# Three moves in an attention and gated-feed-forward kernel: a Silu table load behind two copies, a value cast ahead of a key scaling, and store waits in the order of issue

## The chip, the cores and the metric

The kernel runs on one core of a Trainium2 chip. The metric is the device time of one execution in microseconds. The profile covers the span from the first to the last instruction of one execution; that span is a little shorter than the device time of the same run (271.1 us of 272.93).

## The reference

A linear attention over 8 batches and 8 heads of 576 positions with 64 elements each is followed by a feed-forward layer on the 4608 tokens:

```python
q_s = softmax(q, over the 64 elements)
k_s = softmax(k, over the 576 positions)
kv  = einsum('bhsd,bhse->bhde', k_s, v)
x   = einsum('bhsd,bhde->bhse', q_s, kv), as 4608 tokens x 512
h   = x @ w_in                                # 512 x 2048
g   = h / (1 + exp(-beta * h))                # beta: one per column of h
out = g @ w_out                               # 2048 x 512
```

Each softmax is an exponential divided by its sum (less the maximum, which the kernel does not need).

## The kernel before, in words

**Slabs and passes.** The tokens are worked in nine slabs. Slab t, for t from 0 to 7, holds the first 512 positions of batch t; slab 8 holds the 64 positions left over in each of the eight batches. Each slab has a first pass (x times w_in, 16 tiles of 128 columns, each of four matmuls into one PSUM bank, then a Silu on ScalarE at L746 that writes the bf16 tile GT and a scaling by 1/beta on VectorE at L769) and a second pass (GT times w_out). Slab 0 has a plain second pass (`pass2_group`). The others have `pass2_fast`, which splits the product into two by two blocks and forms them with seven block products in place of eight. These need sums and differences of blocks, made on VectorE (GS1, GS2, WSUM, and at L812 `g_diff`, which overwrites blocks of GT).

**The seven products and their banks.** In `pass2_fast` the products run at L846 in a fixed order on three PSUM banks, s, z5 and z2. After the fourth product z5 holds a finished output quarter, and after the fifth z2 does. ScalarE copies each to O2S (L882, `copy`). Then the sixth product adds to z5 and the seventh to z2, and VectorE adds each of these to TS and writes the last two quarters (L894, `last`). So the sixth and seventh product can't begin to accumulate before the copy of their bank is done. The seventh also reads a block that the second `g_diff` has overwritten.

**Attention.** It is worked one to two slabs ahead and placed between the matmuls of the slab in hand. For a batch: exponentials of q and k on ScalarE (L319), sums and reciprocals for q on VectorE (L357, L359), the product with the reciprocal (L361), a transposition of q, the cast of v to bf16 (`cast_v`, L377, tile VB), the product of keys and values (`kv_steps`), the reciprocal of the key sums (L490) and the scaling of kv with it into KVD (L449 or L459, the "key scaling"), and last the product of KVD and the transposed q, which is copied or cast to XT, the input of the next slab (L511 or L596). Batches 0 and 1 do this with a pair of heads (hp 0 to 3) at a time, from batch 2 on q is transposed by DMA (L606) and four output tiles come from `quad`, in two halves of two tiles (L554).

**What sets the order.** Each engine works its own instructions in the order in which the program adds them; waits between engines are put in by `Program` from what each operation reads and writes. The order is written by hand in two ways. In the first, a list `todo` holds pairs of a due time and a function; `tick` counts matmuls (a pass of a slab is 64 ticks for the first and 64 for the second), and a function is added to the program when its due time is reached. In the second, `pass2_fast` calls hooks: `at(n)` adds what was hung on point n with `on(n, ...)`. Point 4 comes after the copy of z5, point 5 after the copy of z2, point 6 after the addition of z5 and before the seventh product, point 7 at the end.

**ScalarE's table.** The exponential and Silu are in different table sets, and a switch is a table load. `silu_table` runs Silu on one element of a constant tile (DUMMY), so that the load (L1054) is made at that place of the queue and not ahead of the next slab's first real Silu. Slabs 1 and 2 use it in their second pass.

**The end.** The last slab's output goes out as ten stores (`store8`, L790), half issued by SyncE and half by ScalarE. After its last issue SyncE waits for every store's semaphore (L151), so that the program does not end before the data are out. There are twelve such semaphores: `out0` and `out1` for slabs 0 to 7, and ten whose names are built from the output quarter, the half and the tile, for instance `outr0011`.

The hooks of slab 2 and the due times of batch 1 in slab 0 are these lines:

```python
                todo += [(x, one(cast_v, 1, hp, DVE))
                         for hp, x in ((1, 118.5), (2, 123), (3, 127))]
                todo += [(x, steps(kv_steps, 1, (hp,), NOW))
                         for hp, x in enumerate((118, 122, 126))]
...
                on(4, exp_q, 4)
                on(4, silu_table)
                on(4, casts, 4)
                on(6, norm_turn, 4, 0)
```

Of the kernel before, what the change touches and what calls it, by code (L numbers as in the profile page):

```python
# [44 lines left out]
class Program:  # L45
# [83 lines left out]
    def emit(self, nc, es):  # L129
        counts, waits = self.plan()  # L130
        sems = {}
        for key in counts:
            sems[key] = es.enter_context(nc.semaphore("s_" + "_".join(str(x) for x in key)))
        by = {e: [] for e in (PE, ACTE, DVE, POOL, SP)}
        for op, w in zip(self.ops, waits):
            by[op.eng].append((op, w))

        def run(eng):
            def body(h):
                for op, w in by[eng]:  # L140
                    for key, n in w:
                        h.wait_ge(sems[key], n)
                    ins = op.fn(h)
                    if op.slot is not None:
                        ins.then_inc(sems[op.count[0]], 16)
                    elif op.inc:
                        ins.then_inc(sems[op.count[0]], 1)
                if eng == SP:
                    for key, n in sorted(counts.items(), key=str):
                        if key[0] == "dma" and str(key[1]).startswith("out"):  # L150
                            h.wait_ge(sems[key], n)  # L151
            return body

        with nc.Block() as blk:
            for e in (PE, ACTE, DVE, POOL, SP):
                getattr(blk, e)(run(e))


def bass_efficient_attn_shen__then__act_swish_beta_kernel(
# [12 lines left out]
    with ExitStack() as es:  # L172
# [343 lines left out]
        def outr_steps(b):  # L516
            pi = b // 2
            st = {}

            def one(hp, e_):  # L520
                if hp == 0 and e_ == 0:
                    st["b"] = bank()
                bk = st["b"]
                c = hp * 128 + e_ * 64
                d = kd(2 * pi + e_)
                mm(PS[bk][:, c:c + 64], KVD[d][:, hp, :], QTR[:, hp, 64 * e_:64 * e_ + 64],
                   True, True, r=[("kvd", d, hp), "qtr"], w=[("ps", bk)], bk=bk)
                if hp == 3 and e_ == 1:
                    o = bass.AP(XT8, pi * 128, [[NM * SM, 128], [SM, NM], [1, 128]])
                    add(DVE, lambda e: e.tensor_copy(o, PS[bk][:, :]), r=[("ps", bk)],  # L530
                        w=[("xt8", pi, 0), ("xt8", pi, 1)], bank=[bk])
            return [lambda hp=hp, e_=e_: one(hp, e_) for hp in range(NHP) for e_ in range(2)]
# [90 lines left out]
        def one(fn, *a):  # L623
            return lambda: fn(*a)

        def steps(fn, *a):
            return lambda: go(fn(*a))
# [4 lines left out]
        def attn(b):  # L632
            return [(24 if b == 5 else 16, steps(kv_all, b)),
                    (72, one(quad, b, (0, 1), b - 4))]

        def attn_late(b):
            if b < 4:
                x = 100 if b == 2 else 97
                return [(x, steps(kv_all, b)), (x + .1, lambda: g_diff(1)),
                        (118, one(quad, b, (0,)))]  # L640
            return [(96, steps(kv_all, b)), (99, lambda: g_diff(1)), (112, one(quad, b))]

        def spread(steps, lo, hi):
            return [(lo + (hi - lo) * k / len(steps), s) for k, s in enumerate(steps)]
# [310 lines left out]
        for t in range(NSLAB):  # L955
            todo = []
            if t == 0:
                todo = [(x, steps(t_steps, 1, (hp,), NOW, ACTE))
                        for hp, x in enumerate((97, 106, 114, 119))]
                todo += [(107, one(exp_kr_s, 1))]  # L960
                todo += [(x, one(exp_k, 1, hp, 1)) for hp, x in enumerate((108, 115, 120, 125.5))]
                todo += [(x, one(cast_v, 1, hp, DVE))
                         for hp, x in ((1, 118.5), (2, 123), (3, 127))]
                todo += [(x, steps(kv_steps, 1, (hp,), NOW))
                         for hp, x in enumerate((118, 122, 126))]
                todo += [(x, steps(out_step, 1, hp, NOW, ACTE)) for hp, x in enumerate((122.5, 125))]
                todo += [(117, one(o2_evac, 0, 0, 3, ACTE))]
                todo += [(2, steps(out_step, 0, 3, HEAD, DVE))]
            elif t < 4:
                todo = attn_late(t + 1)  # L970
                if t > 1:
                    todo += [(1.5, one(quad, t, (1,)))]
                if t == 3:
                    todo += [(4, one(norm_turn, 4, 2))]
                if t == 1:
                    todo += [(1, steps(out_step, 1, 2, (3,), ACTE)),
                             (3, steps(kv_steps, 1, (3,), (7,))),
                             (6, steps(out_step, 1, 3, (7,), DVE)),
                             (6.1, one(w_sum, 2, 4, 4)), (6.2, one(w_diff, 0)),
                             (6.3, one(w_diff, 1))]  # L980
            elif t < 7:
                todo = attn(t + 1)
            elif t == 7:
                todo = spread(outr_steps(1), 32, 48)
# [59 lines left out]
            def on(n, fn, *a):  # L1044
                hooks.setdefault(n, []).append(lambda: fn(*a))
# [18 lines left out]
            if t == 1:  # L1064
                on(0, exps, 2)
                on(0, casts, 2)
                on(2, norm_turn, 2, 0)
                on(3, norm_turn, 2, 2)
                on(3, g_diff, 0)
                on(4, silu_table)  # L1070
                on(3, load, 4)
            elif t == 2:
                on(0, exps, 3)
                on(2, norm_turn, 3, 0)
                on(3, norm_turn, 3, 2)
                on(3, g_diff, 0)
                on(3, load, 5)
                on(4, exp_q, 4)
                on(4, silu_table)
                on(4, casts, 4)  # L1080
                on(6, norm_turn, 4, 0)
            elif t == 3:
                on(0, exp_k, 4)
                on(0, exp_kr, 4)
                on(0, exp_q, 5)
                on(3, g_diff, 0)
                on(4, norm_turn, 5, 0)
                on(5, norm_turn, 5, 2)
                on(4, exp_qr, 1)
                on(5, exp_k, 5)  # L1090
                on(5, norm_turn_rem)
                on(5, casts, 5)
                on(5, load, 6)
                on(7, load_rem, "qrf", qt_h, QRF, 4)
            elif t + 2 < B:
                b = t + 2
                on(0, exps, b)
                on(0, casts, b)
                if t == 4:
                    on(0, load, 7)  # L1100
                on(3, norm_turn, b, 0)
                on(4, norm_turn, b, 2)
# [40 lines left out]
```

The softmax here doesn't subtract the row's maximum and nothing guards it: scores larger than these inputs give would overflow.

## Time and profile before

| | before |
|---|---|
| time, median of 3 runs | 272.82 us (272.47 to 272.95) |
| span of the profiled run | 271.1 us, 4991 instructions |
| TensorE busy | 262.9 us, 97% |
| VectorE busy | 192.1 us, 71% |
| ScalarE busy | 181.5 us, 67% |
| GpSimd busy | 64.0 us, 24% |
| mean granted TensorE clock | 0.998 |

Busy time is the sum over an engine's instructions; it says how full an engine is, not whether the end waited for it. The chain is the work that ended last, followed back from the last instruction to what released each step. The list of waits says which engine stood still, on which line, and which instruction of which engine it was waiting for. A wait of the busiest engine is a candidate for lost time; one of another engine usually is not. In the timeline each row has the start and the length in us, the engine, the line, the operation, and the tiles written and read; in brackets at the end is the idle time before it with what ended it. PE is TensorE, PEld its weight loads, DVE VectorE, ACT ScalarE, POOL GpSimd, SP SyncE; a q after the name is that engine's queue of instructions that are not compute.

### The profile page before, as it was taken

To read this page: it belongs to the slowest core of one execution; us is meant where nothing else is said; L and a number is where in the kernel's file an instruction comes from. 1 tells how busy PE (TensorE), PEld (TensorE's weight loads), DVE (VectorE), ACT (ScalarE), POOL (GpSimd) and SP (SyncE) were. 2 spreads that over 40 slices of the span, in tenths; PEclk is the share of its full clock that TensorE was granted. 3 is DMA by queue.
4 is the path that set the end of the run, shared out by engine and by line. 5 is a ranking of instruction groups with operands and counts; after the bars stand their busy time and mean duration, and the time that the engine had idled before them with its cause. 6 is when DMAs were issued, how large, how long until landed. Compare 5 with 4: busy or idle time off the path is not lost.

```text
span 271.1 us, 4991 instructions
## 1 busy us (share of the span) xinstructions
PE 262.9 (97%) x1974; PEld 163.7 (60%) x1993; DVE 192.1 (71%) x407; ACT 181.5 (67%) x289; POOL 64.0 (24%) x80
## 2 busy tenths in 40 slices
PE   8999999999999989999999999999999999999994
PEld 2544454448744865477645864587458745874683
DVE  4954586887967798868778876887588458626762
ACT  4998658789468974887778947893883387018610
POOL 2790010006530089000910780036000100000000
PEclk9999999999999999999999999999999999999999
DMA  7999999989699229940489899503600130012005
GB/s 211 322 205 207 225 325 349 301 239 374 160 323 286 82 54 292 281 155 2 81 273 283 265 356 157 182 8 73 213 2 0 41 135 2 0 77 80 0 6 151
DMA packets 59367, 45.95 MB, mean 169 GB/s; under 512 B 28608, under 2 KB 58320, under 8 KB 58320
## 3 DMA queue, kind: packets, MB, share of 16 engines
q1 hardware_dynamic: 54480, 40.90, 53.8%
q0 software_dynamic: 4240, 4.19, 9.3%
q10 hardware_dynamic: 624, 0.53, 0.7%
q8 instruction: 16, 0.26, 0.4%
q14 instruction: 7, 0.06, 0.1%
HBM read 36.71 MB, written 9.44 MB: 170 GB/s over the span
## 4 chain that ended last, share of the span: by engine, by line
PE 85%; DVE 7%; DMA 2%; ACT 2%; SPq 2%; issue 1%; DVEq 0%
PE PS L406 49%; PE PS L846 33%; DMA VF<-in_v_dram 2%; DVE QS L357 2%; PE PS L482 1%; PE PS L554 1%; DVE GT L812 1%; SPq L278 1%; SPq L290 1%; ACT EQ L319 1%; DVE EQ L361 1%; DVE VB L377 1%; DVE QI L359 0%; ACT L1054 0%; ACT O2S L882 0%
## 5 line engine op out<-in xcount | busy, mean ns | idle before, releaser
L406 PE MATMUL PS<-XT,WIN 128*128 128x512 bf16 x560 | 125.3, 379 | 1.2 <-issue 0.3
L746 ACT ACTIVATE GT<-PS,BETA 128x512 bf16<-128x512 f32 x144 | 95.2, 690 | 39.4 <-PE PS L406 39.2
L406 PEld LDWEIGHTS PS<-XT,WIN 128*128 128x128 bf16 x576 | 54.9, 98 | 64.9 <-DVE XT L596 0.7
L769 DVE TENSOR_SCALAR GT<-GT,RB 128x512 bf16<-128x512 bf16 x144 | 52.3, 384 | 39.1 <-ACT GT L746 38.6
L361 POOL TENSOR_TENSOR EQ<-EQ,QI 128x1024 bf16<-128x1024 bf16 (+1 forms) x13 | 25.6, 1968 | 47.2 <-DVE QI L359 46.5
L846 PE MATMUL PS<-WSUM,GT 128*128 128x256 bf16 x256 | 30.1, 273 | 1.2 <-ACT O2S L882 1.0
L846 PE MATMUL PS<-WOUT,GS 128*128 128x256 bf16 x256 | 31.1, 273 | 0.0
L846 PE MATMUL PS<-WOUT,GT 128*128 128x256 bf16 x256 | 29.8, 273 | 0.0
L846 PEld LDWEIGHTS PS<-WSUM,GT 128*128 128x128 bf16 x256 | 24.8, 98 | 5.2 <-issue 1.3
L882 ACT COPY O2S<-PS 128x512 f32<-128x512 f32 (+1 forms) x17 | 9.4, 560 | 26.1 <-PE PS L846 26.0
L846 PEld LDWEIGHTS PS<-WOUT,GT 128*128 128x128 bf16 x256 | 24.8, 98 | 2.9
L846 PEld LDWEIGHTS PS<-WOUT,GS 128*128 128x128 bf16 x256 | 24.8, 98 | 3.0
L319 ACT ACTIVATE EQ<-QF 128x512 bf16<-128x512 f32 x32 | 18.0, 621 | 7.7 <-DMA QF<-in_q_dram 7.6
L805 DVE TENSOR_TENSOR GS<-GT 128x512 bf16<-128x512 bf16 (+2 forms) x32 | 21.9, 685 | 0.0
L377 POOL CAST VB<-VF 128x512 bf16<-128x512 f32 x24 | 16.6, 690 | 22.3 <-DVE GS L805 13.6
L812 DVE TENSOR_TENSOR GT<-GT 128x2048 bf16<-128x2048 bf16 x16 | 21.4, 1362 | 0.0
L357 DVE TENSOR_REDUCE QS<-EQ 128x16 f32<-128x1024 bf16 (+1 forms) x20 | 19.7, 985 | 0.8 <-ACT EQ L319 0.8
L319 ACT ACTIVATE EK<-KF 128x512 bf16<-128x512 f32 x32 | 18.2, 621 | 0.1
L894 DVE TENSOR_TENSOR O2S<-TS,PS 128x512 f32<-128x512 f32 (+1 forms) x17 | 10.7, 647 | 9.7 <-PE PS L846 9.7
L846 PE MATMUL PS<-WSUM,GS 128*128 128x256 bf16 x128 | 16.6, 273 | 0.0
L406 PE MATMUL PS<-WOUT,GT 128*128 128x512 bf16 x62 | 15.0, 379 | 0.1
L846 PEld LDWEIGHTS PS<-WSUM,GS 128*128 128x128 bf16 x128 | 12.5, 98 | 3.2
(90 smaller groups left out, 209.3 us busy)
## 6 DMA issues: line engine op xcount, KB each, us to landing
out_dram<-O2S SPq DMA_DIRECT2D x8, 1024.0 KB, 5.0
QF<-in_q_dram SPq DMA_DIRECT2D x6, 1024.0 KB, 6.5
KF<-in_k_dram SPq DMA_DIRECT2D x6, 1024.0 KB, 9.5
VF<-in_v_dram SPq DMA_DIRECT2D x6, 1024.0 KB, 12.6
KF<-in_k_dram SPq DMA_DIRECT2D x8, 256.0 KB, 5.7
VF<-in_v_dram SPq DMA_DIRECT2D x8, 256.0 KB, 5.7
WOUT<-in_moe_w_out_dram POOLq DMA_DIRECT2D x4, 512.0 KB, 16.4
WIN<-in_moe_w_in_dram POOLq DMA_DIRECT2D x3, 512.0 KB, 9.3
```

The source lines that it names most:

```text
L319: add(ACTE, lambda e, o=o, a=a: e.activation(o, a, ACT.Exp), r=[(name + "f", i, hp)], w=[("e" + name, i, hp)])
L357: add(DVE, lambda e: e.tensor_reduce(s_, a, AX.X, ALU.add), r=ks, w=[("qs", i, hp0)])
L361: add(eng, lambda e: e.tensor_tensor(a, a, vb, ALU.mult), r=ks + [("qi", i, hp0)], w=ks)
L377: add(eng, lambda e: (e.copy if eng == ACTE else e.tensor_copy)(o, a), r=[("vf", i, hp), ("vone", i)], w=[("vb", i, hp)], after=after)
L406: add(PE, lambda e: e.matmul(o, l, r_, start=start, stop=stop), r=r, w=w, bank=[bk])
L746: add(ACTE, lambda e: e.activation(GT[:, f, :], PS[bk][:, :], ACT.Silu, scale=BETA[:, f:f + 1]), r=[("ps", bk), "beta"], w=[("gt", f, 0), ...
L769: add(DVE, lambda e: e.tensor_scalar(GT[:, f, :], GT[:, f, :], RB[:, f:f + 1], None, ALU.mult), r=k + ["rb"], w=k)
L805: add(DVE, lambda e: e.tensor_tensor(GS2[:, i:i + n, :], GT[:, i:i + n, :], GT[:, i + NG:i + NG + n, :], ALU.add), r=[k_ for f in (i, i + ...
L812: add(DVE, lambda e: e.tensor_tensor(gv(f, th, NG), gv(f, th, NG), gv(f, 1 - th, NG), ALU.subtract), r=gk(f, 0, NG) + gk(f, 1, NG), w=gk(f ...
L846: add(PE, lambda e, l=l, r_=r_, st=st, u=u, i=i, b_=b_: e.matmul(PS[b_][:, 256 * u:256 * u + 256], l, r_, start=st, stop=end and i == NG - ...
L882: add(eng, lambda e, b_=b_, u0=u0, u1=u1: (e.copy if eng == ACTE else e.tensor_copy)(o[:, u0:u1, :], bank3(b_)[:, u0:u1, :]), r=[("ps", b_ ...
L894: add(DVE, lambda e, b_=b_, u0=u0, u1=u1: e.tensor_tensor(o[:, u0:u1, :], ts[:, u0:u1, :], bank3(b_)[:, u0:u1, :], ALU.add), r=["ts", ("ps ...
```

## The change

Three places are moved; no operation on data is added or removed.

First, in slab 2 `silu_table` goes from point 4 to point 6. At point 4 it stood, behind four exponentials of batch 4, ahead of the copy of z2. At point 6 it comes after that copy. It is meant to let the copy, and so the seventh product, go without waiting for the table.

Second, in slab 0 the cast of v for pair 1 of batch 1 gets the due time 117.9 in place of 118.5, just ahead of the products of keys and values of pair 0 (118), whose last step adds the reciprocal and the key scaling on VectorE. On VectorE the cast now stands ahead of these two. It is meant to have the cast done by the time that TensorE comes to pair 1.

Third, SyncE's waits for the stores are put in the order in which the last store of each semaphore was issued, in place of the sorted names. It is meant that the last wait is for the store that lands last, with no satisfied waits behind it.

```diff
@@ emit
+        last = {op.count[0]: op.pos for op in self.ops if op.slot is not None}
...
                 if eng == SP:
-                    for key, n in sorted(counts.items(), key=str):
-                        if key[0] == "dma" and str(key[1]).startswith("out"):
-                            h.wait_ge(sems[key], n)
+                    for key in sorted((k for k in counts if str(k[1]).startswith("out")),
+                                      key=lambda k: last[k]):
+                        h.wait_ge(sems[key], counts[key])
@@ slab 0
                 todo += [(x, one(cast_v, 1, hp, DVE))
-                         for hp, x in ((1, 118.5), (2, 123), (3, 127))]
+                         for hp, x in ((1, 117.9), (2, 123), (3, 127))]
@@ slab 2
-                on(4, silu_table)
+                on(6, silu_table)
```

## The prediction

> **What bounds the kernel now.** I read the page's busy shares and chain first, then the list of waits, then the timeline around the three edited places.
>
> ```profile
> PE 262.9 (97%) x1974; PEld 163.7 (60%) x1993; DVE 192.1 (71%) x407; ACT 181.5 (67%) x289; POOL 64.0 (24%) x80
> ...
> PE 85%; DVE 7%; DMA 2%; ACT 2%; SPq 2%; issue 1%; DVEq 0%
> ```
>
> TensorE works 97% of the span, and 85% of the chain is its own matmuls. So an edit is worth what it takes out of TensorE's few gaps, or off the stretch after its last matmul; nothing else moves the end. The list of waits (total us, times, longest) names the gaps that this change can touch:
>
> ```profile
> PE PS L846 <- ACT O2S L882: 1.0, 1, 1.0
> PE PS L406 <- DVE VB L377: 0.3, 1, 0.3
> SPq L151 <- DMA out_dram<-O2S: 1.9, 1, 1.9
> ```
>
> One matmul of a second pass waited 1.0 us for an output copy by ScalarE, one waited 0.3 us for a value cast by VectorE, and SyncE waits for the last stores. The timeline of slab 2 (start us, length us) has the first:
>
> ```profile
> 97.73 2.19 ACT L319 ACTIVATE EQ<-QF 128x512 bf16<-128x512 f32 x4
> 98.99 2.12 DVE L812 TENSOR_TENSOR GT<-GT 128x2048 bf16<-128x2048 bf16 x1
> 99.94 1.28 ACT L1054 ACT_TABLE_LOAD   x1
> 100.69 0.28 PE L846 MATMUL PS<-WSUM,GT 128*128 128x256 bf16 x1
> 101.23 0.20 ACT L1054 ACTIVATE DUMMY<-WARM 128x1 f32<-128x1 bf16 x1
> 101.34 0.57 ACT L882 COPY O2S<-PS 128x512 f32<-128x512 f32 x1
> 101.97 1.92 PE L846 MATMUL PS<-WSUM,GT 128*128 128x256 bf16 x16 [0.99 <-ACT O2S L882]
> 103.47 0.25 DVE L359 RECIPROCAL QI<-QS 128x16 f32<-128x16 f32 x1
> 103.93 0.69 DVE L894 TENSOR_TENSOR O2S<-TS,PS 128x512 f32<-128x512 f32 x1 [0.21 <-PE PS L846]
> 104.72 0.69 DVE L596 CAST XT<-PS 128x512 bf16<-128x512 f32 x1
> ```
>
> The bank z2 has a finished partial product that ScalarE must copy out before the last product accumulates there. Four exponentials and the table load with its dummy (99.94 to 101.34) stand in front of that copy. The second place, around batch 1 at the end of slab 0:
>
> ```profile
> 42.16 0.16 DVE L490 RECIPROCAL RC<-PS 128x1 f32<-128x1 f32 x1
> 42.36 0.35 DVE L449 SCALAR_TENSOR_TENSOR KVD<-PS,RC,MASK 128x128 bf16<-128x128 f32 x1
> 42.62 0.42 DVE L377 CAST VB<-VF 128x512 bf16<-128x512 f32 x1
> ...
> 43.19 0.39 PE L406 MATMUL PS<-VB,EK 128*128 128x131 bf16 x4 [0.30 <-DVE VB L377]
> ```
>
> Three earlier matmuls, begun at 42.08, end 0.81 later, at 42.89; the cast ends at 43.04, so TensorE starts 0.30 late. The third place, the store waits of SyncE:
>
> ```profile
> L151 SPq EVENT_SEMAPHORE  x6: 17/28/1835, 268.5 to 270.7; - x6
> ```
>
> Twelve waits are six instructions. Stepping through them in narrow windows: the second (1.835 us) ends at 270.46, four more follow at 270.49, 270.55, 270.61 and 270.67, and the branch at 270.72.
>
> **What the Trainium skill says.** "ScalarE: Activation LUTs", What ACT_TABLE_LOAD costs: about 1283 ns for the load and 1380 ns of drain, 2.66 us a switch. The trace has the 1.28, but with the dummy only 101.34 - 99.92 = 1.42 us on the queue; I use the trace. The same page, Table sets: the hidden batching unit: copy is in every set, so the copies that now run before the switch need no load of their own; the trace agrees, since copies of slab 3 and later stand between exponentials without a load. "Perfetto Trace Analysis", Identifying Dependency Chains: further waits of one instruction become EventSemaphore instructions; the six above agree.
>
> **The change part by part.**
>
> *Silu table, slab 2: 0.6 us.* The instruction order of the changed kernel puts copy z2, then the first XT copy of the next slab, then load and dummy, then the second XT copy. Copy z2 goes to 99.94 and ends at 100.51. That removes this wait, but two others stand behind it. First, the last product reads what the subtraction L812 writes, done at 98.99 + 2.12 = 101.11. In slab 1 the same subtraction (70.70 + 2.12 = 72.82) let TensorE go at 72.96, 0.14 later. So TensorE restarts at 101.25, not at 100.8 where the previous product's matmuls end: 101.97 - 101.25 = 0.72 gained, not the 0.99 of the wait. Second, the third of the next slab's four input tiles is cast by VectorE (L596, 104.72 to 105.41), behind the last addition L894. VectorE is not free to follow by 0.72: its queue runs without a hole from 98.99 to the reciprocal at 103.47. After such a reciprocal the next operation began 0.17 later (94.88 to 95.05), and PSUM operations of this size follow each other by 0.60 (101.03, 101.63). So addition at 103.64, cast at 104.24, done 104.93, weight load 0.06 later at 104.99 (before, 105.41 to 105.47). TensorE would want that matmul at 105.67 - 0.72 = 104.95 (before, the third tile's first matmul follows one at 105.46 by 0.21) and gets it at about 105.05. Gain 0.62; bounds 0.48, if the matmul follows its weights as closely as before (105.47 to 105.67), and 0.72.
> The table load does not come back elsewhere: the first XT copy waits for the matmuls L554 (done 100.76), ends near 101.4, load and dummy end near 102.9, and the second XT copy waits for matmuls that end at 103.9 in the new order. ScalarE was idle 2.39 us there. The transposed tile of these matmuls, issued at 100.1, landed 3.1 later, at 103.2; they now come at 103.5. Further on in slab 3 nothing takes the gain: ScalarE sat idle 1.17 us before its first Silu and VectorE 0.44 before its first scaling, both for want of TensorE's results.
>
> *Second value cast earlier: 0.3 us.* The cast of pair 1 goes ahead of the reciprocal and the key scaling KVD of pair 0. Its one new risk is its load, behind which both now queue, and TensorE's output matmul of pair 0 behind them:
>
> ```profile
> VF<-in_v_dram SPq DMA_DIRECT2D x1, 256.0 KB, 5.4
> ```
>
> That is the issue at 36.75, landed 36.75 + 5.4 = 42.15 (42.10 to 42.20 by rounding); VectorE reaches the cast at 42.16. So it waits 0 to 0.07 us, ends near 42.6, and TensorE starts its next matmul when the three earlier ones end, at 42.89: 0.30 gained. Behind it: a cast passes VectorE on after 0.34 (40.62 to 40.96), so reciprocal 42.53, KVD 42.73 to 43.08; the output matmul, 43.69 before, wants it at 43.39. The changed kernel adds a wait to this matmul; it is met 0.3 earlier. The following links move together: the loads of pairs 2 and 3 landed at 38.00 + 5.6 = 43.6 and 39.02 + 6.1 = 45.1, their casts would come at 43.85 and 45.43. From there on the chain of the page is TensorE, VectorE and ScalarE up to the end, with no transfer of fixed time, so the 0.30 stays. Bounds 0 (a load on time only for its old place) and 0.30.
>
> *Store waits: 0.2 us.* Before, names were sorted, so four instructions follow the wait that lasts. In order of issue the last instruction holds the two last stores. They were issued at 267.83 and 268.3, with 2.4 and 2.1 us to landing: 270.2 and 270.4, so the last wait ends between 270.46 and 270.52 and the branch moves from 270.72 to about 270.52. Bounds 0.15 and 0.24.
>
> Sum: 0.62 + 0.30 + 0.20 = 1.12 us; 272.82 - 1.12 = 271.70. The profile's fixed rest (272.93 for a span of 271.1) is taken unchanged.
>
> **The rivals.**
>
> *The cast waits for its load.* Margin is about zero, and transfers of this group took 5.4 to 6.1 us. If it lands 0.4 later, the gain of this part is gone: 272.82 - 0.82 = 272.0. For it: the margin. Against it: the transfers in this stretch move 348 to 352 GB/s in each microsecond from 41 on, so 256 KB take 0.75 us, and 40.59 + 2 x 0.75 gives 42.09.
>
> *The slab 2 gain is taken by a next wait.* VectorE already takes 0.1 of it by my sum; if its queue runs as late as before (cast at 104.72), no more than 0.1 is left, and with the other parts 272.82 - 0.1 - 0.3 - 0.2 = 272.2, with a weaker cast 272.4. For it: VectorE without a hole for 5 us. Against: the 0.21 us that it waited for TensorE before L894 is a hole, and the cast also waited for L554.
>
> *Slower.* The table load, moved to the place after the first XT copy, delays the second one, and the early cast blocks VectorE. The load has 103.9 - 102.9 = 1.0 us to spare; if the first XT copy were so late that none were left, 1.4 us minus this 1.0 would be lost, 0.4. A load landing at 43.2 instead of 42.15 would put the output matmul at about 44.2 against 43.69, 0.5 lost. Both, less the 0.2 of the waits, 273.5. Nothing in the profile speaks for it but the thin margin of one load.
>
> **How the numbers follow.** Forecast 271.70 with 0.62; late cast 272.0 with 0.17; slab 2 gain lost, about 272.35, 0.16; slower 0.05. A tenth of a per cent is 0.27 us and three runs before spread over 0.48, so the forecast, taken with its bounds, is from 272.82 - 1.26 to 272.82 - 0.63: 271.6 to 272.2, with noise 271.2. Range 271.2 to 272.4. The 0.2% line is at 272.27: forecast and late cast lie below it, 0.79; lost gain within, 0.16; slower 0.05.
>
> **What would show it.** Slab 2: copy z2 straight after the exponentials, the wait on O2S gone, and a wait of about 0.25 on GT L812 ahead of the 16 matmuls in its place; the third tile's weight load waiting longer than 0.33 for XT L596. Batch 1: no wait of L406 on VB L377. End: no store wait after the long one. Wrong would be: a wait on VF ahead of the second cast, a ScalarE copy waiting behind the load, or a gain that is there at the first matmul of slab 3 and gone by that of slab 4.

## The result and the profile after

The changed kernel takes 271.69 us (median of 6 runs, 271.43 to 271.96), beside 272.88 for the kernel before: ratio 0.9956 with a 95% interval of 0.9943 to 0.997, that is 1.2 us less (0.8 to 1.6). The forecast was 271.70. The span of the profiled run is 270.0 us, 1.1 less.

Cut at the first matmul of each slab's first pass, the profiles of the two kernels differ so: 0.38 us less in slab 0 (30.24 for 30.62), 0.15 more in slab 1 (29.58 for 29.43), 0.72 less in slab 2 (28.30 for 29.02), 0.18 more in slab 3 (28.20 for 28.02), nothing in slabs 4 to 7 (109.39 in both), and 0.33 less from slab 8's first matmul to the end (29.45 for 29.78). The gain lies where the three moves are, and 0.33 us of it are given back in slabs 1 and 3. (Some profiles lack the record of the very first matmul of a pass; the first, here and below, is from slab 2 on the first that all profiles have, which is the second of the pass.)

The page of the changed kernel: TensorE's busy time is about what it was, and its share of the chain is larger.

```profile
PE 262.4 (97%) x1974; PEld 163.4 (60%) x1993; DVE 192.9 (71%) x407; ACT 181.4 (67%) x289; POOL 63.1 (23%) x80
...
PE 87%; DVE 6%; POOL 2%; issue 1%; DMA 1%; ACT 0%; POOLq 0%; DVEq 0%
```

(The changed kernel's lines have numbers one higher than before.) In its list of waits, the wait of the second-pass matmuls on the copy O2S and that of L407 on the cast VB are gone; of TensorE's other waits, the first and the last of these have grown (from 0.7, longest 0.3, and from 0.2), and the second is new:

```profile
PEld PS L407 <- DVE XT L597: 0.8, 2, 0.5
...
PE PS L555 <- DMA QT<-EQ: 0.6, 1, 0.6
...
PE PS L847 <- DVE GT L813: 0.3, 1, 0.3
```

The new one is in slab 1, where TensorE waits for a transposition of q by DMA; it comes back under the fourth experiment.

**Slab 2**, the timeline of the changed kernel around the seventh product:

```profile
97.53 2.19 ACT L320 ACTIVATE EQ<-QF 128x512 bf16<-128x512 f32 x4
...
98.78 2.12 DVE L813 TENSOR_TENSOR GT<-GT 128x2048 bf16<-128x2048 bf16 x1
99.62 0.57 ACT L883 COPY O2S<-PS 128x512 f32<-128x512 f32 x1
...
100.50 0.28 PE L847 MATMUL PS<-WSUM,GT 128*128 128x256 bf16 x1
100.70 0.59 ACT L597 CAST XT<-PS 128x512 bf16<-128x512 f32 x1 [0.51 <-PE PS L555]
...
101.05 1.91 PE L847 MATMUL PS<-WSUM,GT 128*128 128x256 bf16 x16 [0.27 <-DVE GT L813]
101.30 1.28 ACT L1055 ACT_TABLE_LOAD   x1
...
103.43 0.63 DVE L895 TENSOR_TENSOR O2S<-TS,PS 128x512 f32<-128x512 f32 x1
...
103.86 0.59 ACT L597 CAST XT<-PS 128x512 bf16<-128x512 f32 x1 [1.06 <-PE PS L555]
103.98 0.68 DVE L597 CAST XT<-PS 128x512 bf16<-128x512 f32 x1
...
104.71 1.19 PEld L407 LDWEIGHTS PS<-XT,WIN 128*128 128x128 bf16 x7 [0.50 <-DVE XT L597]
104.71 0.39 PE L407 MATMUL PS<-XT,WIN 128*128 128x512 bf16 x1
```

The copy follows the exponentials at once. The single matmul ahead of the seventh product starts at 100.50 and the product at 101.05: 0.55 us, where before it was 1.28 (100.69 to 101.97). What is left is the wait on the subtraction L813. The table load stands behind the first XT cast, and ScalarE is still idle 1.06 us before the second. At the third input tile the weight load now waits 0.50 us for VectorE's cast (0.33 before), and the matmul that uses it starts with it at 104.71: 0.39 after the matmul before it, where the others of this stretch are 0.22 apart.

**Batch 1**, the timeline of the changed kernel:

```profile
42.13 0.42 DVE L378 CAST VB<-VF 128x512 bf16<-128x512 f32 x1
42.18 0.81 PE L407 MATMUL PS<-WOUT,GT 128*128 128x512 bf16 x3
...
42.66 0.35 DVE L450 SCALAR_TENSOR_TENSOR KVD<-PS,RC,MASK 128x128 bf16<-128x128 f32 x1
...
42.83 0.39 PE L407 MATMUL PS<-VB,EK 128*128 128x131 bf16 x4
```

The cast shows no wait for its load, and pair 1's first matmul starts 0.65 after the three before it did (1.11 before).

**The end.** The last addition now ends at 267.04 and SyncE's branch comes at 269.64, 2.60 later (2.92 before). The six wait instructions fall at 268.18, 268.50, 268.70, 268.96, 269.38 and 269.56: each lets go as one of the last six stores lands, and the branch follows the last one by 0.08.

### The profile page after: what moved, and what is told of

It is laid out like the page before. It is cut to its first block, busy times and chain, and to the rows that moved or that the text cites. A ratio compares the mean times of both kernels' runs of the same rounds, so it can differ in the third digit from the quotient of the medians.

```text
span 270.0 us, 4991 instructions
## 1 busy us (share of the span) xinstructions
PE 262.4 (97%) x1974; PEld 163.4 (60%) x1993; DVE 192.9 (71%) x407; ACT 181.4 (67%) x289; POOL 63.1 (23%) x80
## 4 chain that ended last, share of the span: by engine, by line
PE 87%; DVE 6%; POOL 2%; issue 1%; DMA 1%; ACT 0%; POOLq 0%; DVEq 0%
PE PS L407 54%; PE PS L847 30%; DVE QS L358 2%; PE PS L555 1%; DMA QT<-EQ 1%; DVE GT L813 1%; PE PS L483 1%; POOL VB L378 1%; POOL EQ L362 1%; PE PS L405 1%; DVE EQ L362 1%; DVE QI L360 0%; POOL VR L392 0%; DVE XT L512 0%; DVE TS L916 0%
## 5 line engine op out<-in xcount | busy, mean ns | idle before, releaser
L407 PE MATMUL PS<-XT,WIN 128*128 128x512 bf16 x560 | 125.6, 379 | 1.3 <-issue 0.3
L407 PEld LDWEIGHTS PS<-XT,WIN 128*128 128x128 bf16 x576 | 54.8, 98 | 65.4 <-DMA WIN<-in_moe_w_in_dram 0.9
L770 DVE TENSOR_SCALAR GT<-GT,RB 128x512 bf16<-128x512 bf16 x144 | 52.9, 388 | 38.3 <-ACT GT L747 37.5
L813 DVE TENSOR_TENSOR GT<-GT 128x2048 bf16<-128x2048 bf16 x16 | 21.8, 1386 | 0.0
L378 POOL CAST VB<-VF 128x512 bf16<-128x512 f32 x24 | 15.6, 652 | 22.0 <-DVE GS L806 13.2
L407 PE MATMUL PS<-WOUT,GT 128*128 128x512 bf16 x62 | 15.0, 379 | 0.1
```

Of the source, the lines that this page charges most:

```text
L378: add(eng, lambda e: (e.copy if eng == ACTE else e.tensor_copy)(o, a), r=[("vf", i, hp), ("vone", i)], w=[("vb", i, hp)], after=after)
L407: add(PE, lambda e: e.matmul(o, l, r_, start=start, stop=stop), r=r, w=w, bank=[bk])
L770: add(DVE, lambda e: e.tensor_scalar(GT[:, f, :], GT[:, f, :], RB[:, f:f + 1], None, ALU.mult), r=k + ["rb"], w=k)
L813: add(DVE, lambda e: e.tensor_tensor(gv(f, th, NG), gv(f, th, NG), gv(f, 1 - th, NG), ALU.subtract), r=gk(f, 0, NG) + gk(f, 1, NG), w=gk(f ...
```

## The experiments

The reading of each rests on intervals within its trace, since the time of pair 0's cast, and with it all that follows, lay between 40.24 and 41.03 us in the profiles, whatever the kernel.

**The Silu table alone** (on the kernel before).

```diff
-                on(4, silu_table)
+                on(6, silu_table)
```

> Only the move of the Silu table in slab 2. Theory (three separate gains): the wait of the seventh product on the copy O2S is replaced by a wait on the subtraction, 0.7 us are gained at the first matmul of slab 3, 0.17 of that is lost at its third tile for VectorE's cast, 0.55 us less than before in all, about 272.3; the first transposition of slab 1 lands 3.1 us after its issue, as before. Rival (the three edits help each other): less than 0.3 us or more than 0.8 us.

272.4 us, ratio 0.998 (0.9971 to 0.9989), so 0.55 us less (the medians differ by 0.48). In the trace the seventh product again starts 0.55 after the single matmul (101.11 to 101.66); slab 3's first pass, from its first matmul to the first of its second pass, takes 14.23 us (103.62 to 117.85) where the kernel before took 14.06 (103.94 to 118.00). 0.73 gained and 0.17 lost are 0.56. The transposition of slab 1 landed after 3.1 us. The theory holds. The profiled execution itself was longer, 272.1 us of span, for other reasons: pair 0's cast came 0.4 us later, and the last four stores landed 3.6 to 4.2 us after their issue, where the kernel before had 2.1 to 2.7.

**The cast alone** (on the kernel before).

```diff
-                         for hp, x in ((1, 118.5), (2, 123), (3, 127))]
+                         for hp, x in ((1, 117.9), (2, 123), (3, 127))]
```

> Only the earlier cast of pair 1. Theory: 0.36 to 0.47 us are gained at pair 1's first matmul, and in the second pass of slab 1 some 0.15 to 0.3 of them are given back, since the transposition of q, issued 0.36 us earlier, meets the end of slab 0's store and takes about 3.7 us instead of 3.1; 0.2 us less than before in all, about 272.6. Rival (the longer transposition was chance): it takes 3.1 us here too, the gain of about 0.4 stays up to the end, about 272.4.

272.43 us, ratio 0.9991 (0.998 to 1.0002): about 0.25 less by the ratio, 0.45 by the medians, not clear of nothing by time alone. In the trace, pair 1's first matmul comes 2.14 us after the start of pair 0's cast (40.52 to 42.66), where it was 2.57 in the kernel before and in the kernel with the table alone. The transposition took 3.3 us, neither the 3.7 of the theory nor the 3.1 of the rival, and it cost nothing: from pair 1's first matmul to slab 2's first, 31.73 us, as in the kernel before (43.19 to 74.92). The give-back that the changed kernel's first profile shows (31.88 us, with a landing after 3.7) is not in this one.

**The store waits alone** (on the kernel before).

```diff
-                    for key, n in sorted(counts.items(), key=str):
...
+                    for key in sorted((k for k in counts if str(k[1]).startswith("out")),
+                                      key=lambda k: last[k]):
```

> Only the order of the store waits. Theory: the time from the end of the last addition to SyncE's branch becomes shorter by 0.2 to 0.3 us and nothing else changes, about 272.6. Rival (satisfied waits cost nothing, and the shorter end in the changed kernel came from earlier landings): no change, 272.8.

272.69 us, ratio 0.9992 (0.9979 to 1.0006): unclear by time. In the trace it takes 2.65 us from the end of the last addition to the branch, and 0.08 from the letting go of the last wait to the branch. The cast alone, which keeps the old order, is the fair partner:

```profile
L151 SPq EVENT_SEMAPHORE  x6: 17/28/1854, 267.8 to 270.0; - x6
```

Its long wait lets go at 269.75 and four more instructions follow at 269.80, 269.86, 269.92 and 269.98; the branch is at 270.04, 0.29 after. So 0.21 us is what the order is worth. The kept traces say the same from the landing of the last store: the branch comes 0.32 us after it in the three kernels with the old order and 0.08 to 0.09 after it in the eight with the new one (the kernel with more waits, below, apart), a difference of 0.23. The rest of the difference of 2.92 and 2.60 is the issue and the landing of the last stores.

**Slab 0's store behind the loads of slab 1** (on the changed kernel).

```diff
                     o2_evac(0, n // 3, 3 + n // 3, ACTE)
-                    if n == 10:
-                        store(0)
...
                 on(3, load, 4)
+                on(3, store, 0)
```

> The changed kernel with slab 0's store issued after the transpositions and the loads of slab 1, not ahead of them. Theory (the transposition of slab 1 collided with this store): it takes 3.1 us again, and the first matmul of slab 2 comes 0.15 us earlier than in the changed kernel, about 271.5. Rival (it collided with the loads of batch 3, or it was chance): no change against the changed kernel, 271.7.

271.68 us, ratio 0.9954 (0.9942 to 0.9966), the changed kernel's time. The transposition landed after 3.1 us and the interval from pair 1 to slab 2 was 31.73. That fits the theory, but the changed kernel run once more (below) has the same without the move, so this run alone does not show that the store was the cause. The twelve profiles together speak for it. Where the store landed at most 2.2 us after the issue of the transposition (five profiles), the transposition took 3.14 or 3.15 us; where it landed later (2.35 to 2.48 us after, and 2.82 in the first profile of the changed kernel), the transposition landed 0.86 to 0.91 us after the store, and so took 3.3 to 3.7. In the two kernels with the store moved it took 3.14 and 3.15. The loads, the rival, are not needed for this: one of them still landed 1.3 us after the issue in the kernel of this experiment, and the transposition took 3.15.

**The sums of batch 4 behind the input casts** (on the changed kernel).

```diff
-                on(6, norm_turn, 4, 0)
...
-                    todo += [(4, one(norm_turn, 4, 2))]
+                    todo += [(2, one(norm_turn, 4, 0)), (4, one(norm_turn, 4, 2))]
```

> The changed kernel with the sums and reciprocals of batch 4's first two pairs (one reduction and one reciprocal of VectorE, some 1.4 us) moved from point 6 of slab 2 to just after the two last input casts of slab 3. Theory (the gain of slab 2 is cut by VectorE's queue at the third tile): the weight load's wait on the cast XT falls from 0.50 to about 0.33 us, and from the seventh product's first matmul of slab 2 to slab 3's second pass TensorE needs 0.17 us less; about 271.5. Rival (the cast waits for TensorE's matmuls L555 anyway): the same interval as in the changed kernel, 271.7; or the sums now delay the first scaling of GT, and it is longer.

The timeline of this kernel:

```profile
102.91 0.69 DVE L895 TENSOR_TENSOR O2S<-TS,PS 128x512 f32<-128x512 f32 x1 [0.90 <-PE PS L847]
...
103.70 0.69 DVE L597 CAST XT<-PS 128x512 bf16<-128x512 f32 x1
...
104.45 1.63 PEld L407 LDWEIGHTS PS<-XT,WIN 128*128 128x128 bf16 x9 [0.33 <-DVE XT L597]
```

VectorE now stands idle 0.90 us before the addition, the cast follows TensorE's matmuls, and the weight load waits 0.33 again. Slab 3's first pass takes 14.06 us (102.92 to 116.98), the 0.17 is back. By time, 271.87 us (ratio 0.9964, 0.9953 to 0.9975), not to be told from the changed kernel. The theory of VectorE's queue is shown; its gain is below what the runs vary by.

**The load of pair 1's values one place later** (on the changed kernel; each number is a pair of heads, for batch 1 alone).

```diff
-            for c in range(NHP):
-                load_main("kf", kt_h, KF, b, split=4, cs=(c,))
-                load_main("vf", vt_h, VF, b, split=4, cs=(c,))
+            for n, c in ((("k", 0), ("v", 0), ("k", 1), ("k", 2), ("v", 1), ("v", 2), ("k", 3), ("v", 3))
+                         if b else [(n, c) for c in range(NHP) for n in "kv"]):
+                load_main(*(("kf", kt_h, KF) if n == "k" else ("vf", vt_h, VF)), b, split=4, cs=(c,))
```

> The changed kernel with the load of batch 1's values for pair 1 issued after the keys of pair 2, so that it lands one transfer (about 0.75 us) later. Theory (the early cast has no margin on its load): the cast waits some 0.6 to 0.7 us for VF, with the reciprocal and the key scaling of pair 0 behind it, pair 1's first matmul starts 0.5 to 0.7 us later than in the changed kernel, and this stays up to the end: about 272.3. Rival (the load lands with room to spare, or slack behind takes it up): less than 0.2 us more, 271.8.

```profile
42.60 0.43 DVE L378 CAST VB<-VF 128x512 bf16<-128x512 f32 x1 [0.63 <-DMA VF<-in_v_dram]
...
43.14 0.35 DVE L450 SCALAR_TENSOR_TENSOR KVD<-PS,RC,MASK 128x128 bf16<-128x128 f32 x1
...
43.17 0.39 PE L407 MATMUL PS<-VB,EK 128*128 128x131 bf16 x4 [0.32 <-DVE RC L491]
```

The cast waits 0.63 us for its load, and pair 1's first matmul comes 2.83 after pair 0's cast (40.34 to 43.17), 0.6 to 0.7 later than the 2.11 to 2.25 of the other kernels with the early cast. The median is 272.39, 0.7 more than the changed kernel (ratio to before 0.9979, 0.9967 to 0.9992). So the early cast lives on a load that comes just in time, and one transfer of delay costs as much as the cast gains and more.

**The twelve store waits three times** (on the changed kernel).

```diff
                         h.wait_ge(sems[key], counts[key])
+                    for _ in range(2):
+                        for key in sorted((k for k in counts if str(k[1]).startswith("out")),
+                                          key=lambda k: last[k]):
+                            h.wait_ge(sems[key], counts[key])
```

> The changed kernel with the twelve store waits made three times, so that 24 satisfied waits, in twelve instructions, follow the last landing. Theory (each satisfied pair costs about 0.06 us): SyncE's branch comes 0.7 us later after the last landing than in the changed kernel, about 272.4. Rival (satisfied waits are nearly free): less than 0.2 us.

```profile
L156 SPq EVENT_SEMAPHORE  x18: 17/28/28, 268.2 to 270.2; - x18
```

The last wait for a landing lets go at 269.46, the twelve others follow each 0.06 after the one before up to 270.18, and the branch is at 270.24: 0.78 after, where the changed kernel has 0.08. The time of the single run is 272.46 us. A satisfied wait instruction costs 0.06 us here.

**No early table load in slab 2** (on the changed kernel).

```diff
-                on(6, silu_table)
```

> The changed kernel without the early table load in slab 2: the load stands where the first Silu of slab 3 needs it. Theory (the load costs only by what waits behind it; ScalarE stands idle 1.34 us ahead of that Silu, the load takes 1.28): the first Silu starts at most 0.1 us later, and the time is that of the changed kernel, 271.7. Rival (a load without the preload is paid in full, 1.3 us or more): 273.0.

```profile
103.82 0.59 ACT L597 CAST XT<-PS 128x512 bf16<-128x512 f32 x1 [2.57 <-PE PS L555]
...
104.42 1.28 ACT L747 ACT_TABLE_LOAD   x1
...
105.74 1.85 ACT L747 ACTIVATE GT<-PS,BETA 128x512 bf16<-128x512 f32 x3
```

The load stands just ahead of the first Silu and fills the idle time there. Slab 3's first pass takes 14.23 us (102.97 to 117.20), as in the changed kernel (103.01 to 117.24); 272.03 us, ratio 0.9967 (0.9955 to 0.9979), which overlaps the changed kernel's interval. The rival's 1.3 us are not there.

**Both further moves in one kernel (store and sums), and the changed kernel again, unedited.**

> The changed kernel with both further moves: batch 4's first sums behind the input casts of slab 3, and slab 0's store behind the loads of slab 1. Theory: 0.17 us less than the changed kernel in slab 3's first pass, the transposition of slab 1 back at 3.1 us; about 271.5, and 0.1 to 0.3 us less than the changed kernel run beside it. Rival (these moves are below what the start of the kernel varies by): no difference in time, though the intervals in the trace are shorter.

> The changed kernel once more, beside the last version on the same chip: 271.7. If the long transposition of its first profile was chance, the interval from pair 1's first matmul to slab 2's first is 31.73 us as in the other kernels; if it belongs to the change, it is 31.88 again.

With both moves 271.68 us (ratio 0.9965, 0.9951 to 0.9978); the changed kernel beside it 271.92 (0.9961, 0.995 to 0.9972). The trace has the 14.06 us of slab 3 and a transposition of 3.1 us, but no gain over the changed kernel is shown in time. In the second profile of the changed kernel the transposition landed after 3.1 us and the interval from pair 1 to slab 2 is 31.73 (42.70 to 74.43).

## Why the prediction was right, step by step

The sum was 1.12 us and came out as 1.2; the three parts were sized apart, and two of them missed, in opposite directions.

*Silu table, 0.62 forecast, 0.55 measured.* The step that the removed wait has a second wait behind it, on the subtraction, was right to the hundredth: 0.72 forecast, 1.28 less 0.55 is 0.73 measured, and 0.72 to 0.74 in the other profiles with the move. VectorE's queue was named as the next limit and is (the move of the sums gives 0.17 back). The term mis-sized is the loss at the third input tile, 0.10 in my sum and 0.17 measured. The sum has TensorE want that tile's first matmul at 105.67 less 0.72. But the matmul starts together with its weight load, and in the kernel before that was at 105.47:

```profile
105.47 0.10 PEld L406 LDWEIGHTS PS<-XT,WIN 128*128 128x128 bf16 x1 [0.33 <-DVE XT L596]
105.47 0.39 PE L406 MATMUL PS<-XT,WIN 128*128 128x512 bf16 x1
```

It followed the matmul before it by 0.22, so the 0.33 us that the weight load waited cost TensorE nothing then. In the terms of the sum it was wanted at 104.75, not at 104.95, and with the weight load at 104.99 the loss would have been 0.24. The cast came earlier than I had summed: with the seventh product at 101.05 in place of 101.25, the weight load was due at 104.79, and it came at 104.71. That leaves about the 0.17 measured. So the 0.62 was this close in part because two errors of mine went against each other. The table load was hidden where it was said to be.

*The earlier cast, 0.30 forecast, 0.32 to 0.46 measured at its place.* The mis-sized term is "TensorE starts its next matmul when the three earlier ones end, at 42.89". That end is a modelled one, and matmuls overlap: the next starts 0.65 after the first of the three (42.18 to 42.83), not 0.81. "TensorE: Matmul & The Clock Gate", Back-to-back issue gap, in the Trainium skill has N/2.4 + 2.5 ns for a single matmul, 216 ns at 512 columns, and says that for a stream of matmuls this is too much (131 ns measured); in this trace the three start 0.216 us apart, which is the formula's figure and not the lower one. Three times that is 0.65. So before, TensorE lost about 0.46 there and not the 0.30 of the idle column.

How much of it comes back differs from one execution to the next, since it depends on which is later, the load of pair 0 or TensorE. Counted from those three matmuls, pair 1 came 0.15, 0.46 and 0.61 us late in the three profiles with the cast in its old place, and 0 to 0.15 late in the eight with the early cast and the loads in their place. From pair 0's cast to pair 1's matmul it was 2.57 in the two traces with the cast in its old place in which VectorE sets the pace (the store-wait kernel, where TensorE came late, has 2.86), and 2.11 to 2.25 in those eight. The margin of the load was nil, as said, and the load was on time each time.

The sentence that there is "no transfer of fixed time" from there on was too strong: in one of the two profiles of the changed kernel the transposition of slab 1 took 3.7 us and cost 0.15 of the gain. It took 3.1 to 3.4 us in all other profiles, and up to 3.4 the interval to slab 2 was the same. TensorE, and with it the transposition, comes earlier for the earlier cast and meets more of slab 0's store in flight, which fits all twelve profiles as the cause (fourth experiment).

*Store waits, 0.20 forecast, 0.21 to 0.23 measured,* in the traces. The cost of a satisfied wait, read off four instructions, held for twelve. One link was not as written: the last two stores are not in one instruction. They landed at 269.4 and 269.55, and the fifth and the sixth instruction let go at 269.38 and 269.56. The sum does not change by it.

*What came from chance.* The forecast agrees with the median to 0.01 us, closer than either can be known: the medians of the changed kernel in its two sets of runs are 271.69 and 271.92.

## What to carry to other kernels

When a wait is to be removed, look for the next one behind it before the gain is written down: here the 0.99 us on the copy was worth 0.73, then 0.55, and both limits could be read from the timeline of the old kernel. In this kernel a table load cost only by what was queued behind it; look for a place where its engine is idle. An operation moved ahead on its engine takes along the wait for its load, so check the landing as well as the gain. A wait of a weight load is not yet a loss: see whether the matmul behind it starts later after the one before it than its neighbours do.

## What the runs showed that was not expected

The idle column of the matmul rows understates a gap: a row's length is its modelled end (0.38 us for 512 columns), while the next matmul can start 0.215 after it; the gap at pair 1 was 0.46, shown as 0.30. The same program starts its steady part up to 0.8 us earlier or later from one profile to the next, by when the first loads of batch 1 land, which may be why gains of 0.2 us were seen in intervals of the trace and not in the times. The end varies too. The last four stores of one execution landed 3.6 to 4.2 us after their issue against 2.1 to 2.8 in others. And ScalarE's third issue of these stores took 0.6 us in seven profiles and 0.9 to 1.3 in five, which puts off its last store: in the second profile of the changed kernel the branch came 2.98 us after the last addition, no sooner than in the kernel before, though only 0.08 to 0.09 after the last landing.
